# The second FFN's output as seven half-size products over pairs of features

## The chip, the cores and the metric

One core of a Trainium2 chip runs the kernel. The metric is the device time of one execution in microseconds (us); of the kernel before it is 911.15 us, the median of three runs (910.92 to 911.19). The engines are TensorE (PE, matrix products, with its weight loads shown as PEld), VectorE (DVE), ScalarE (ACT), GpSimd (POOL) and SyncE (SP), which issues nearly all transfers.

## The reference

Attention over a window of 64 positions, an FFN with ELU, and an RMS-normalized gated FFN, all in float32, on 2304 tokens of width 512:

```python
x = attention(q, k, v)                 # 4 batches, 8 heads, 576 positions, head width 64
h = x @ w_in                           # 512 -> 2048
g = np.where(h > 0.0, h, np.exp(np.minimum(h, 0.0)) - 1.0)
x = g @ w_out                          # 2048 -> 512
xn = x / np.sqrt(np.mean(x * x, axis=-1, keepdims=True) + 1e-06) * rms_g
g = xn @ w_gate                        # 512 -> 1536
silu = g * (1.0 / (1.0 + np.exp(-g)))
out = (silu * (xn @ w_val)) @ w_out2   # 1536 -> 512
```

## The kernel before

Products run in float32r, a rounded float32. To keep float32's accuracy each operand is split into a high part and a low part (the rest), and a product of two operands is three matmuls: high by high, high by low, low by high. A split is a copy with rounding (ACT or DVE) and a subtraction (DVE or POOL).

**First FFN.** Tokens go in five blocks (384, 384, 512, 512, 512). For each of 16 features f of 128, in_steps computes h (12 matmuls, L704) and g, and out_steps adds g's share to four accumulators (12 matmuls, L781), two steps later (LAG). Attention for later blocks runs between these steps. While blocks 1 to 3 run, prep_steps reads w_gate and w_val, forms the sums that the second FFN needs, splits them (put_out) and stores them in DRAM (pspill). prep_out does the same for w_out2 without sums: 12 features, one matrix each, two splits of 256 columns each, six in the last block and six in the first superblock (ospill). norm_steps normalizes a finished block.

**Second FFN.** Three superblocks (sb) of 768 tokens, in two token blocks of 384. pair(sb, i) computes g for features i and i + 6 at once: a 2x2 by 2x2 block product with Winograd's seven products instead of eight (ORDER), each for gate and value (qi), six matmuls of 384 columns each (L1106). The results are collected in SBUF (keep on ACT, L1061; plus on DVE, L1066), multiplied (times, L1070) and split into high and low (L1092, L1094). After three pairs, outs(sb, h) multiplies the g of six features with w_out2, plainly: for each of six token tiles of 128, six features and three terms, so 108 matmuls of 512 columns (L1148), four features first and the last two after. emit1 copies the first half's accumulators to SBUF (L1294), emit2 adds the second half's to them (L1300) and stores the rows (L1302). x_items forms the sums and splits of x for the next superblock.

**Order.** Every operation is a step with costs per engine that are written by hand, what it reads and writes, and the tile it needs. Plan runs a list scheduler over all steps: among the steps that could start first on an engine it takes the one with the longest chain of costs behind it (tail). Its order on each engine is then fixed, SP's transfers too. Places per tile kind are in LIMITS; of the kind "wu" (32 places of 4 KB per partition) are first the first FFN's weights and then x, g, the loaded sums of w_gate and w_val (p_load, 512 KB each) and w_out2 (o_load). A transfer is put into the program at a numbered point of its superblock (put, after).

Of the kernel before, what the change touches and what calls it, by code (L numbers as in the profile page):

```python
# [8 lines left out]
F32 = mybir.dt.float32  # L9
# [12 lines left out]
LIMITS = dict(w=4, c=6, e2=3, y=4, wu=32, kT=1, kq=1, vw=2, s=2, st=3, e=2, g=3, x0=1, x1=1, xt=1,  # L22
# [7 lines left out]
class Plan:  # L30
# [9 lines left out]

    def add(self, costs, fn, reads=(), writes=(), load=0.0, rows=128, name=None):
        x = Step()
        x.costs = {e: c * self.MARGIN.get(e, 1.0) for e, c in costs.items()}
# [67 lines left out]
    def could(self, x, e):  # L111
# [6 lines left out]
        for tile in x.tiles:  # L118
            if tile not in self.live and tile[0] in LIMITS:
                new.setdefault(tile[0], set()).add(tile)  # L120
# [15 lines left out]
    def put(self, x, e, t):  # L136
        c = x.costs[e]
        for tile in x.tiles:
            tag = tile[0]
            if tile not in self.live:  # L140
                self.live[tile] = len(self.users[tile])
                if tag in LIMITS:
                    if self.used.get(tag, 0) < LIMITS[tag]:
                        self.used[tag] = self.used.get(tag, 0) + 1
                    else:
                        self.freed[tag].remove(min(self.freed[tag]))
# [10 lines left out]
        for tile in x.tiles:  # L157
            self.live[tile] -= 1
            if not self.live[tile]:
                self.freed.setdefault(tile[0], []).append(  # L160
                    max(self.end[u] for u in self.users[tile]))
        self.order.append((x, e))

    def run(self, given=()):
# [13 lines left out]
        while ready:  # L178
# [36 lines left out]
def kernel(  # L215
# [459 lines left out]
    def load_step(f, i, tile):  # L675
        add({"SP": 0.55}, lambda e: f.load(i + 1), writes=[tile], load=1.45,
# [258 lines left out]
    def put_out(dst, dkey, src, key, sg):  # L935


        def tile_():
            return get((*sg, 0), lambda: mp.tile(
                [128, 2, 256], F32R, tag="stg", name="stg", bufs=2))  # L940
# [3 lines left out]
        add({"POOL": 0.76}, lambda e: nc.gpsimd.tensor_tensor(  # L944
# [5 lines left out]
    def prep_steps(t):  # L950

        i, qi = t // 2, t % 2
        raw = [("big4", ("r", 2 * t + j), 0) for j in range(2)]
        m = [(f"wm{j}", ("p", 2 * t + j)) for j in range(2)]
# [8 lines left out]
        for j in range(2):  # L963
            load_step(fwp, 2 * t + j, raw[j])
        for j in range(2):
            def join(e, j=j):
                held[(*m[j], 0)] = fwp.join(2 * t + j)
            add({"POOL": 0.8}, lambda e, j=j: fwp.s1(2 * t + j), reads=[raw[j]], writes=[one])
# [3 lines left out]
        def comb(out, okey, in0, in1, keys, op=ALU.subtract):  # L972
            add({"POOL": 0.76}, lambda e: nc.gpsimd.tensor_tensor(
                out=out(), in0=in0(), in1=in1(), op=op), reads=keys, writes=[okey])
# [3 lines left out]
        def put(j, src, key):  # L978
            put_out(pspill[:, 7 * i + ORDER.index(j), qi * 512:(qi + 1) * 512]
                    .rearrange("p (a c) -> p a c", a=2), ("dram", ("p", 7 * i + ORDER.index(j)), qi),  # L980
                    src, key, ("stg", (t, j)))

# [12 lines left out]
    def prep_out(j):  # L995

        n, f = 4 * NP2 + j, OF[j]
        raw, m = ("big4", ("r", n), 0), (f"wm{n % 2}", ("p", n))
        one = ("wm2", "top", 0)

        def join(e):
            held[(*m, 0)] = fwp.join(n)

        load_step(fwp, n, raw)
        add({"POOL": 0.8}, lambda e: fwp.s1(n), reads=[raw], writes=[one])
        add({"DVE": 0.75}, join, reads=[raw, one], writes=[(*m, c) for c in range(2)])
        for h in range(2):
            put_out(ospill[:, f, :].rearrange("p (a c) -> p a c", a=2)
                    [:, :, h * 256:(h + 1) * 256], ("dram", ("o", f), h),
# [350 lines left out]
```

## Time and profile before

| | us |
|---|---|
| median of three runs (lowest to highest) | 911.15 (910.92 to 911.19) |
| the profiled execution | 911.7 |
| its span, first to last instruction | 909.3 |
| PE busy | 896.3 (99%) |
| DVE busy | 547.9 (60%) |
| ACT busy | 460.5 (51%) |
| POOL busy | 227.5 (25%) |
| matmuls of the output phases (L1148), 648 of them | 103.0 + 52.9 |
| matmuls of the pairs (L1106), 1512 of them | 121.1 + 80.9 + 40.7 + 40.3 |

The profile is one execution, taken in hardware. Busy is the union of an engine's records; the records of matmuls overlap, since one begins before the one ahead has drained, so a matmul's own duration (390 ns for 512 columns) is longer than its share of the time. [...]

### The profile page before, as it was taken

Reading aid. Unit: us, or ns where it says so; the run is one execution under the profiler, and the core shown is the slowest. Engines: PE = TensorE matmul, PEld = TensorE weight load, DVE = VectorE, ACT = ScalarE, POOL = GpSimd, SP = SyncE. Lnnn points to the kernel's source line nnn. Section 1 sums busy time; section 2 is a strip of 40 time slices with the busy share of each in tenths; the row PEclk is TensorE's granted clock in tenths of the full one; section 3 lists DMA queues with packets and bytes.
Section 4 is the critical chain, followed back from the end, with each engine's and each line's share of the span. In section 5 each row is a group of like instructions: output and inputs, shape, how many; then the busy total and the mean of one; then the engine's idle time right before and its main releaser. Section 6 shows DMA issues by size and latency. Waiting matters only on the chain.

```text
span 909.3 us, 15448 instructions
## 1 busy us (share of the span) xinstructions
PE 896.3 (99%) x5577; PEld 805.8 (89%) x5577; DVE 547.9 (60%) x1188; ACT 460.5 (51%) x1118; POOL 227.5 (25%) x270
## 2 busy tenths in 40 slices
PE   8899999999999999999999999999999999999998
PEld 7889999998887888888888998998998998998996
DVE  6899967656555557557744781694560584560561
ACT  6788676666556665657445542451432451432430
POOL 3777631434434442344142013100000000000000
PEclk9999999999999999999999999999999999999999
DMA  9996226844385453945595529978947638847611
GB/s 228 324 325 155 58 82 184 221 129 140 122 240 145 142 151 106 254 141 160 200 353 176 199 72 338 367 276 322 338 139 270 210 112 314 310 140 272 214 48 69
DMA packets 149915, 182.89 MB, mean 201 GB/s; under 512 B 81744, under 2 KB 109392, under 8 KB 149840
## 3 DMA queue, kind: packets, MB, share of 16 engines
q1 hardware_dynamic: 149840, 181.91, 62.3%
q8 instruction: 44, 0.72, 0.3%
q14 instruction: 31, 0.25, 0.1%
HBM read 144.13 MB, written 37.75 MB: 200 GB/s over the span
## 4 chain that ended last, share of the span: by engine, by line
PE 88%; DMA 3%; DVE 3%; SPq 3%; ACT 1%; issue 1%; POOL 0%; DVEq 0%; ACTq 0%; POOLq 0%
PE y L781 19%; PE w L704 18%; PE y L1106 16%; PE w L1106 12%; PE y L1148 11%; PE w L1148 5%; SPq L308 2%; PE w L534 2%; PE w L455 1%; SPq L642 1%; PE w L519 1%; DVE wm L655 1%; PE w L400 1%; DMA kq<-in_q_dram 1%; DMA big<-in_moe_w_val_dram 1%
## 5 line engine op out<-in xcount | busy, mean ns | idle before, releaser
L781 PE MATMUL y<-g,wu 128*128 128x512 f32 (+1 forms) x960 | 213.5, 372 | 2.5 <-POOL wu L671 1.7
L704 PE MATMUL w<-x,wu 128*128 128x512 f32 (+1 forms) x960 | 213.0, 372 | 0.8 <-ACT x L559 0.5
L704 PEld LDWEIGHTS w<-x,wu 128*128 128x128 f32 x960 | 173.4, 188 | 26.1 <-issue 2.2
L781 PEld LDWEIGHTS y<-g,wu 128*128 128x128 f32 x960 | 173.0, 188 | 26.1 <-POOL wu L671 2.1
L1106 PE MATMUL y<-xw,pu 128*128 128x384 f32 x648 | 121.1, 334 | 0.0
L1066 DVE TENSOR_TENSOR c<-c,w 128x384 f32<-128x384 f32 x72 | 39.9, 554 | 133.5 <-PE w L1106 128.7
L1106 PEld LDWEIGHTS y<-xw,pu 128*128 128x128 f32 x648 | 113.2, 188 | 0.5 <-issue 0.2
L1148 PE MATMUL y<-wu,g 128*128 128x512 f32 x432 | 103.0, 390 | 0.0
L1148 PEld LDWEIGHTS y<-wu,g 128*128 128x128 f32 x432 | 81.0, 188 | 16.6
L944 POOL TENSOR_TENSOR stg<-wm,stg 128x256 fp32r<-128x256 f32 x72 | 58.8, 817 | 127.2 <-ACT stg L942 127.2
L1106 PE MATMUL w<-xw,pu 128*128 128x384 f32 x432 | 80.9, 334 | 0.0
L746 DVE SCALAR_TENSOR_TENSOR e<-e,w 128x512 f32<-128x512 f32 (+1 forms) x80 | 50.3, 631 | 50.5 <-ACT e L744 50.1
L752 DVE TENSOR_TENSOR g<-e,g 128x512 fp32r<-128x512 f32 (+1 forms) x80 | 66.1, 828 | 22.9 <-ACT g L750 22.4
L1106 PEld LDWEIGHTS w<-xw,pu 128*128 128x128 f32 x432 | 75.4, 188 | 0.1
L742 ACT ACTIVATE e<-w 128x512 f32<-128x512 f32 (+1 forms) x80 | 44.2, 552 | 61.5 <-PE w L704 60.5
L1061 ACT COPY c<-y 128x384 f32<-128x384 f32 x72 | 34.4, 479 | 59.8 <-PE y L1106 58.6
L648 POOL CAST top<-big 128x512 f16<-128x512 bf16 x36 | 29.6, 821 | 126.1 <-DMA big<-in_moe_w_out_dram 68.5
L1084 ACT ACTIVATE e<-c 128x384 f32<-128x384 f32 x54 | 28.4, 526 | 63.1 <-DVE c L1066 62.9
L1070 DVE TENSOR_TENSOR e<-e,c 128x384 f32<-128x384 f32 x108 | 59.3, 562 | 0.5
L1148 PE MATMUL w<-wu,g 128*128 128x512 f32 x216 | 52.9, 389 | 0.0
L671 POOL TENSOR_TENSOR wu<-wm,wu 128x512 fp32r<-128x512 f32 x32 | 49.4, 1566 | 13.8 <-ACT wu L666 10.7
L750 ACT CAST g<-e 128x512 fp32r<-128x512 f32 (+1 forms) x73 | 42.0, 577 | 20.9 <-DVE e L746 20.5
(132 smaller groups left out, 1213.8 us busy)
## 6 DMA issues: line engine op xcount, KB each, us to landing
pu<-pspill SPq DMA_DIRECT2D x126, 512.0 KB, 5.6
pspill<-stg SPq DMA_DIRECT2D x84, 256.0 KB, 2.1
wu<-ospill SPq DMA_DIRECT2D x36, 512.0 KB, 4.1
tmp<-in_moe_w_out_dram SPq DMA_DIRECT2D x16, 511.8 KB, 8.3
tmp<-in_moe_w_in_dram SPq DMA_DIRECT2D x16, 511.0 KB, 7.9
vw<-in_v_dram SPq DMA_DIRECT2D x27, 256.0 KB, 4.2
ospill<-stg SPq DMA_DIRECT2D x24, 256.0 KB, 4.5
big<-in_moe_w_out_dram SPq DMA_DIRECT2D x12, 511.8 KB, 5.3
```

The costliest lines, as they stand in the source:

```text
L671: nc.gpsimd.tensor_tensor(out=u[:, 1, :], in0=m, in1=u[:, 0, :].bitcast(F32), op=ALU.subtract)
L704: nc.tensor.matmul(pt[:, :n], lhsT=wt[:, a, kk * 128:(kk + 1) * 128], rhs=xs[kk][:, c, :n], start=(i == 0), stop=(i == len(seq) - 1))
L742: add({"ACT": of_n(0.49, n)}, lambda e: nc.scalar.activation(out=et(), in_=ph(), func=AF.Relu, scale=-1.0), reads=ws, writes=[e_])
L746: add({"DVE": of_n(0.56, n)}, lambda e: nc.vector.scalar_tensor_tensor(out=et(), in0=et(), scalar=-1.0, in1=ph(), op0=ALU.add, op1=ALU.max ...
L750: lambda e: copy_on(e)(out=gt()[:, 0, :n], in_=et()),
L752: add({"DVE": of_n(0.68 if b else 0.93, n)}, lambda e: nc.vector.tensor_tensor(out=gt()[:, 1, :n], in0=et(), in1=gt()[:, 0, :n].bitcast(F3 ...
L781: nc.tensor.matmul(py[m][:, :n], lhsT=wt[:, a, m * 128:(m + 1) * 128], rhs=g[:, c, :n], start=(first and i == 0), stop=(last and i == 2))
L944: add({"POOL": 0.76}, lambda e: nc.gpsimd.tensor_tensor(out=tile_()[:, 1, :], in0=src(), in1=tile_()[:, 0, :].bitcast(F32), op=ALU.subtrac ...
L1066: add({"DVE": 0.55}, lambda e: nc.vector.tensor_tensor(out=c_of(ck), in0=c_of(ck), in1=at(bk), op=ALU.add), reads=[bk], writes=[ck])
L1070: add({"DVE": 0.55}, lambda e: nc.vector.tensor_tensor(out=et(), in0=et(), in1=src_of(sk), op=ALU.mult), reads=[sk], writes=[ek])
L1106: nc.tensor.matmul(at(bk), lhsT=p_of(sb, i, j)[:, qi, a, kk * 128:(kk + 1) * 128], rhs=X_of(sb, j, kk)[:, x, :], start=(first and n == 0), ...
L1148: nc.tensor.matmul(at(m), lhsT=g[:, a, (m % 3) * 128:(m % 3 + 1) * 128], rhs=w[:, x, :], start=(f == fs[0] and i == 0), stop=(f == fs[-1] ...
```

## The change

- The output phase outs multiplies by seven products too. The 2x2 blocks are features i and i + 6 by the two token blocks (g), and features by the two halves of 256 output columns (w_out2). For each of the seven products j, in ORDER, a sum or difference of blocks of g is formed (source, 0 or 1 subtraction per pair), split (split), and multiplied: three token tiles, three pairs, three terms, 27 matmuls of 256 columns, as two steps (q): two token tiles in a bank of tag y, the third in one of tag w. Accumulators are shared along the products as in pair, and each step's result is collected at once (keep, plus). g itself is kept whole in float32, and pair no longer splits it.
- Differences and low parts may go to DVE (cost 0.56) or POOL (1.2). Sums for even products sit in the three places of tag g, for odd ones in three of big4 (in the first half of the first superblock in wu). The steps on a pair's g are ready as soon as that pair's g is, so during the next pair.
- prep_out now forms w_out2's seven sums of quarters per pair of features and splits and stores them (44 places of 256 KB instead of 24 stores). Four pairs come in the last block of the first FFN, two in the first superblock.
- o_load loads two such sums at a time, 11 loads per half instead of 6. Loaded weights (p and o) get their own limit of 8 of wu's 32 places.
- The planner takes, of DVE and POOL, the engine that would end a step sooner; preparation and normalization get a higher priority (sooner); accumulators of tag y are given out in order.
- Results are collected per half of columns and stored as 256 or 128 tokens by 256 columns, eight stores per superblock instead of six.

The core of the diff:

```diff
-LIMITS = dict(w=4, c=6, e2=3, y=4, wu=32, kT=1, ...
+LIMITS = dict(w=4, c=6, e2=3, y=4, wu=32, wl=8, kT=1, ...
...
     def queue(self, t):
         if t[0] == "wu":
-            return "raw" if t[1][0] == "r" else "wu" if isinstance(t[1], tuple) else None
+            return ("raw" if t[1][0] == "r" else "wl" if t[1][0] in ("p", "o") else
+                    "wu" if isinstance(t[1], tuple) else None)
+        if t[0] == "y" and isinstance(t[1][0], int):
+            return "y"
         return None if t[0] in "wy" else t[0]
+    def tags(self, t):
+        return (t[0], "wl") if self.queue(t) == "wl" else (t[0],)
...
                 can = {e: self.could(x, e) for e in x.costs}
+                if len(can) == 2 and "POOL" in can and "DVE" in can and can["DVE"] is not None:
+                    e = min(can, key=lambda e: can[e] + x.costs[e])
+                    can = {e: can[e]}
...
-                        per.setdefault(e, []).append((t, -self.tail[x.index], x.index))
+                        per.setdefault(e, []).append((t, -self.tail[x.index] - x.early, x.index))
...
     def pair(sb, i, after):
...
             times(ek, et, sk)
-            f, blk = i + NP2 * (pos // 10 - 1), pos % 10 - 1
...
-            add({"ACT": 0.52, "DVE": 0.42}, lambda e: copy_on(e)(
-                out=g_of(gkey)[:, 0, :], in_=et()), reads=[ek], writes=[(*gkey, "h")])
-            add({"DVE": 0.56}, lambda e: nc.vector.tensor_tensor(
-                out=g_of(gkey)[:, 1, :], in0=et(), in1=g_of(gkey)[:, 0, :].bitcast(F32),
-                op=ALU.subtract), reads=[ek, (*gkey, "h")], writes=[(*gkey, "l")])
...
-        for m in range(NM):
-            mm(m, fs[:-2])
-            after()
-        for m in range(NM):
-            mm(m, fs[-2:])
-            emit(m, po[m], lambda m=m: at(m))
-            after()
+    def outs(sb, h, after, emit):
+        us = [3 * h + ii for ii in range(3)]
...
+        def minus(o, x, y):
+            add({"DVE": 0.56, "POOL": 1.2}, lambda e: on(e).tensor_tensor(
+                out=o[0](), in0=x[0](), in1=y[0](), op=ALU.subtract),
+                reads=[v[1] for v in (x, y) if v[1] != o[1]], writes=[o[1]])
+        def S_key(jp, i, part):
+            return (("g", "wu" if sb + h == 0 else "big4")[jp % 2], ("S", sb, i, jp), part)
...
+        def split(jp, i, src):
+            add({"ACT": 0.52, "DVE": 0.42}, lambda e: copy_on(e)(
+                out=S_of(jp, i)[:, 0, :], in_=src[0]()),
+                reads=[src[1]], writes=[S_key(jp, i, "h")])
+            add({"DVE": 0.56, "POOL": 1.2}, lambda e: on(e).tensor_tensor(
+                out=S_of(jp, i)[:, 1, :], in0=src[0](),
+                in1=S_of(jp, i)[:, 0, :].bitcast(F32), op=ALU.subtract),
+                reads=[src[1], S_key(jp, i, "h")], writes=[S_key(jp, i, "l")])
+        def source(j, i):
+            if j == 5:
+                minus(G(i, 0, 0), G(i, 0, 1), G(i, 0, 0))
+            elif j == 6:
+                minus(t2(i), G(i, 1, 1), G(i, 0, 0))
+            elif j == 7:
+                minus(G(i, 0, 1), G(i, 1, 1), G(i, 0, 1))
+            elif j == 4:
+                minus(G(i, 1, 0), G(i, 1, 0), t2(i))
+            return {1: G(i, 0, 0), 5: G(i, 0, 0), 6: t2(i), 2: G(i, 1, 0), 7: G(i, 0, 1),
+                    3: G(i, 1, 1), 4: G(i, 1, 0)}[j]
...
+        for jp, j in enumerate(ORDER):
+            for i in us:
+                split(jp, i, source(j, i))
+            for q in range(2):
...
+                    for m in ((0, 1), (2,))[q]:
+                        for ii, i in enumerate(us):
+                            w = o_of(sb, o_entry(i, j))
+                            for n, (a, x) in enumerate(((0, 0), (0, 1), (1, 0))):
+                                nc.tensor.matmul(
+                                    at(bk)[:, (m % 2) * 256:(m % 2) * 256 + 256],
+                                    lhsT=S_of(jp, i)[:, a, m * 128:(m + 1) * 128],
+                                    rhs=w[:, x * 256:(x + 1) * 256],
...
+                add({"PE": (2.16, 1.08)[q]}, product, reads=reads, writes=[bk])
+                emit(j, q, bk, (lambda bk=bk: at(bk)))
+                after()
...
+    PREP = [{}, *[{f: 4 * b + n for n, f in enumerate((3, 6, 9, 12))}
+              for b in range(nblk - 2)],
+            {5: 12, 8: 13, 11: 14, 13: 15}]
...
+        def emit1(j, q, bk, at, keep=keep, plus=plus):
+            (plus if j in (2, 7, 3) else keep)(STEP[j][0], q, bk, at)
+        def emit2(j, q, bk, at, plus=plus, store=store):
+            plus(STEP[j][0], q, bk, at)
+            if STEP[j][1]:
+                store(STEP[j][0], q)
```

## Rows read from the trace of the kernel before

**Rows 1.** The page: span, and TensorE's busy time, share and instructions.

```profile
span 909.3 us, 15448 instructions
...
PE 896.3 (99%) x5577; PEld 805.8 (89%) x5577; DVE 547.9 (60%) x1188; ACT 460.5 (51%) x1118; POOL 227.5 (25%) x270
```

**Rows 2.** Windows: busy us and instructions per engine, granted clock, DMA share, GB/s.

```profile
410.00:492.00 82.00, 82.00 (x362) 67.51 (x361) 52.40 (x80) 44.32 (x86) 27.03 (x31) 1.00 0.63 215
495.00:632.00 137.00, 137.00 (x723) 127.96 (x722) 86.96 (x161) 57.81 (x123) 14.74 (x18) 1.00 0.74 263
562.00:606.00 44.00, 44.00 (x253) 43.52 (x252) 26.75 (x53) 22.07 (x49) 5.73 (x7) 1.00 0.97 358
632.00:769.00 137.00, 137.00 (x724) 128.42 (x723) 69.83 (x137) 49.23 (x103) 0.00 (x0) 1.00 0.66 230
769.00:905.00 136.00, 136.00 (x720) 127.58 (x719) 59.35 (x116) 42.84 (x88) 0.00 (x0) 1.00 0.52 182
```

**Rows 3.** TensorE's timeline, one output phase: start us, duration us, engine, line, op.

```profile
605.82 2.24 PE L1106 MATMUL y<-x,pu 128*128 128x384 f32 x12
607.90 2.92 PE L1148 MATMUL y<-wu,g 128*128 128x512 f32 x12
610.66 2.88 PE L1148 MATMUL w<-wu,g 128*128 128x512 f32 x12
613.38 2.88 PE L1148 MATMUL y<-wu,g 128*128 128x512 f32 x12
...
632.42 1.75 PE L1106 MATMUL y<-xw,pu 128*128 128x384 f32 x9
```

**Rows 4.** The page, costliest groups: count, busy us, mean ns of one, idle before.

```profile
L1148 PE MATMUL y<-wu,g 128*128 128x512 f32 x432 | 103.0, 390 | 0.0
...
L1148 PE MATMUL w<-wu,g 128*128 128x512 f32 x216 | 52.9, 389 | 0.0
...
L1148 PEld LDWEIGHTS y<-wu,g 128*128 128x128 f32 x432 | 81.0, 188 | 16.6
```

**Rows 5.** TensorE's timeline, transposes and the product after them.

```profile
161.08 1.03 PE L519 MATMUL w<-ident,s 128*128 128x128 f32 x8
161.96 0.60 PE L400 MATMUL w<-ident,kq 128*128 128x128 f32 x4
162.31 2.33 PE L704 MATMUL w<-x,wu 128*128 128x384 f32 x12
```

**Rows 6.** Timeline of the weight loads in the same stretch.

```profile
162.28 2.04 PEld L704 LDWEIGHTS w<-x,wu 128*128 128x128 f32 x12
```

**Rows 7.** VectorE's timeline, a dense stretch; nine operations from first to last start.

```profile
613.08 1.02 DVE L902 TENSOR_TENSOR xw<-slot,xw 128x384 fp32r<-128x384 f32 x2
...
617.30 1.02 DVE L909 TENSOR_TENSOR slot<-slot,slot 128x384 f32<-128x384 f32 x2
```

**Rows 8.** Groups of VectorE from 495 to 909 us: count, busy us, mean ns.

```profile
L1300 DVE TENSOR_TENSOR slot<-slot,y 128x512 f32<-128x512 f32 x12 | 8.3, 688 | 33.3 <-PE y L1148 33.3
...
L655 DVE SCALAR_TENSOR_TENSOR wm<-big,top 128x512 int32<-128x512 int32 x6 | 4.1, 690 | 12.8 <-POOL top L648 8.1 <-POOL stg L944 4.6
...
L839 DVE SCALAR_TENSOR_TENSOR big<-big,g_sb,big 128x512 f32<-128x512 f32 x4 | 3.9, 987 | 0.0
```

**Rows 9.** Groups of GpSimd, whole span.

```profile
L944 POOL TENSOR_TENSOR stg<-wm,stg 128x256 fp32r<-128x256 f32 x72 | 58.8, 817 | 127.2 <-ACT stg L942 127.2
L671 POOL TENSOR_TENSOR wu<-wm,wu 128x512 fp32r<-128x512 f32 x32 | 49.4, 1566 | 13.8 <-ACT wu L666 10.7 <-DMA kq<-in_k_dram 3.1
```

**Rows 10.** Groups of VectorE, 26 to 185 us (only L746 reads PSUM).

```profile
L752 DVE TENSOR_TENSOR g<-e,g 128x384 fp32r<-128x384 f32 x30 | 28.4, 953 | 5.9 <-ACT g L750 5.7
L746 DVE SCALAR_TENSOR_TENSOR e<-e,w 128x384 f32<-128x384 f32 x30 | 16.3, 548 | 10.6 <-ACT e L744 10.4
```

**Rows 11.** DMA issues from 495 to 909 us: count, KB, median us to landing.

```profile
pu<-pspill SPq DMA_DIRECT2D x109, 512.0 KB, 6.0
wu<-ospill SPq DMA_DIRECT2D x36, 512.0 KB, 4.1
```

**Rows 12.** Timeline of the end: last matmuls and the last add.

```profile
902.61 2.88 PE L1148 MATMUL y<-wu,g 128*128 128x512 f32 x12
...
905.53 0.69 DVE L1300 TENSOR_TENSOR slot<-slot,y 128x512 f32<-128x512 f32 x1 [0.67 <-PE y L1148]
```

More of the change, by code (lines that the diff above doesn't have):

```diff
@@ L119, in could @@
             if tile not in self.live and tile[0] in LIMITS:
-                new.setdefault(tile[0], set()).add(tile)
+                for tag in self.tags(tile):
+                    new.setdefault(tag, set()).add(tile)
         for tag, ts in new.items():
@@ L981, in put, with sums, comb @@
                     src, key, ("stg", (t, j)))
+        sums(q4, k4, both, sk, put, {"POOL": 0.82})
+    def sums(q4, k4, both, sk, put, cost):
+        def comb(out, okey, in0, in1, keys, op=ALU.subtract):
+            add(cost, lambda e: on(e).tensor_tensor(
+                out=out(), in0=in0(), in1=in1(), op=op), reads=keys, writes=[okey])
         put(1, q4[0, 0], k4[0, 0])
@@ L1235 @@
             if f == 4:
-                next(norm, None)
+                plan.sooner(100.0, lambda: next(norm, None))
             if f < F1:
@@ L1242 @@
                 attention(u, b=max(i for i in range(nblk) if FIRST_U[i] <= u))
-            if b and f in (3, 6, 9, 12) and not last:
-                prep_steps((b - 1) * 4 + (3, 6, 9, 12).index(f))
+            if f in PREP[b]:
+                kind, i = preps[PREP[b][f]]
+                plan.sooner(40.0, lambda: (prep_steps if kind == "p" else prep_out)(i))
             for fn in slots.get(f, ()):
@@ L1278 @@
             next(norm)
-            put(4, lambda: next(norm, None))
-            for j in range(F2 // 2, F2):
-                put(6 + 2 * (j - F2 // 2), lambda j=j: prep_out(j))
+            put(2, lambda: plan.sooner(100.0, lambda: next(norm, None)))
+            for i in range(4, NP2):
+                put(2 * (i - 4), lambda i=i: plan.sooner(0.0, lambda: prep_out(i)))
         if sb + 1 < NSB:
-            put(36, lambda: x_load(sb + 1))
+            put(38, lambda: x_load(sb + 1))
             for j, fn in enumerate(x_items(sb + 1)):
-                put(48 + j, fn)
+                put(50 + j, fn)
@@ new lines, in keep, with plus @@
+        def keep(pos, q, bk, at, sb=sb, part=part, p_key=p_key):
+            n = (512, 256)[q]
+            add({"ACT": (0.59, 0.38)[q], "DVE": (0.69, 0.42)[q]}, lambda e: copy_on(e)(
+                out=part(pos, q), in_=at()[:, :n]), reads=[bk], writes=[p_key(pos, q)])
+        def plus(pos, q, bk, at, sb=sb, part=part, p_key=p_key):
+            n = (512, 256)[q]
+            add({"DVE": (0.69, 0.42)[q]}, lambda e: nc.vector.tensor_tensor(
+                out=part(pos, q), in0=part(pos, q), in1=at()[:, :n], op=ALU.add),
+                reads=[bk], writes=[p_key(pos, q)])
@@ new lines, in store @@
+        def store(pos, q, sb=sb, part=part, p_key=p_key):
+            tok, c = 2 * NB * sb + NB * (pos % 10 - 1) + 256 * q, 256 * (pos // 10 - 1)
+            n = (256, 128)[q]
+            add({"SP": 0.55}, lambda e: nc.sync.dma_start(
+                out=out[tok:tok + n, c:c + 256].rearrange("(m p) c -> p m c", p=128),
+                in_=part(pos, q).rearrange("p (m c) -> p m c", c=256)),
+                reads=[p_key(pos, q)], load=0.7)
+        STEP = {1: (11, 0), 5: (22, 0), 6: (12, 0), 2: (11, 1), 7: (22, 1), 3: (12, 1), 4: (21, 1)}
```

227 lines of the change are left out of this document (124 added, 103 removed).

## The prediction

> **What bounds the kernel now.** I read the page first. TensorE (PE) is busy 896.3 of 909.3 us [rows 1], but busy time is an average over stages, so the next view was the windows of the stage that is changed, the second FFN from about 495 us on. In each of the three parts of that stage PE is busy for the whole window (137.00 of 137.00), at the full granted clock (1.00, the 2.4 GHz level), while VectorE (DVE) has 87.0, 69.8 and 59.4 us of work and ScalarE (ACT) 57.8, 49.2 and 42.8 [rows 2]. The last block of the first FFN, in which most of the new preparation is placed, is as full: 82.00 of 82.00 [rows 2]. So matmul time taken out of the second FFN comes off the end one for one, unless PE has to wait for something it does not wait for now. The rest of the argument is the price of the new matmuls, and then who could be late.
>
> **The matmuls.** A half's output phase now runs from 607.90 to 632.42 us: 24.52 us [rows 3] for 108 matmuls of 512 columns (648 in six halves, [rows 4]), and in its steady part 12 of them take 2.72 us (610.66 to 613.38), 226.7 ns each. Twelve of 384 columns in the pair before it take 2.08 us (605.82 to 607.90), 173.3 ns each [rows 3]. The two lie on a line of 53.3 ns per 128 columns, so 256 columns should cost 120.0 ns. The change issues 7 products x 3 token tiles x 3 pairs x 3 terms = 189 matmuls a half: 22.68 us. That is 1.84 us less per half and **11.0 us less in all**. Only that: an eighth of the streaming (648 x 213.3 ns = 138.2 us) is 17.3, and the 13.3 ns that the line leaves at zero columns, paid 1134 times instead of 648, takes 6.5 of it back; the first matmuls of a phase, a little dearer now, make up the difference.
>
> No row shows a 256-column product of this type, so I bound it. Every matmul has a weight load of its own, and its record lasts 188 ns [rows 4]. Were that the time for which the loader is taken, the price would be 188, and the change would add 1134 x 188 - 147100 ns = 66 us. But the loads of the pairs already come every 173.3 ns, so the record is longer than the load. Closer is what happens after transposes, whose products follow each other every 108 ns (eight take 1.03 us, four 0.60): the last four end at 162.56, the weights of the next product begin to load at 162.28, under the last transpose [rows 6], and the twelve products of 384 columns behind them end at 164.64, exactly 12 x 173.3 ns after the transposes [rows 5]. A load of 128 columns is thus hidden behind a product of 108 ns, and a product of 256 columns lasts 120. I take 120.0, with 120 to 126 in the range (6 ns is what reading two-digit starts can hide), worth 0 to +6.8 us. [...]
>
> **The work of VectorE.** Dense, DVE starts a 384-column operation every 0.469 us (613.08 to 617.30, nine of them), although each record lasts 0.55 [rows 7]; an operation of 512 columns lasts 0.688 [rows 8], so about 0.60 dense, and one of 256, by the same line, 0.33. Per superblock (768 tokens) the splits of g go from 24 to 42 and 24 differences are new: 42 x 0.469 = 19.7 us. Collecting the sums goes from 6 adds of 512 columns (3.6 us) to ten of 512 and ten of 256 (9.3): +5.7. DVE comes to 69.8 + 25.4 = 95 us in a superblock of 133. The 18 added copies on ACT are hidden (49 + 9 of 133). On average all of it is covered; places where it is not:
> - *The opening, pairs 0 to 2 and the first output phase, 66 us.* DVE has 42 operations of pairs (19.7), 33 of sums and splits (15.5), the normalization of the last block with four at 0.99 and twelve at 0.69 (12.2), four joins at 0.69 (2.8) [rows 8] and the collecting (2.8): 53 us. Fits by 13. Beside it GpSimd (POOL) has the last two preparations of w_out, 13 operations each, about 0.82 us apiece [rows 9]: 21 us.
> - *The boundary between superblocks, pair 5, second output phase, next pair 0, 52 us.* 28 operations of pairs (13.1), 23 sums and splits that could not begin earlier (10.8), collecting and adding (6.5), 22 for the next x (10.3): 41 us. Fits by 11.
>
> Here the planner's new rule matters: a sum or a low half goes to POOL whenever POOL would end it sooner. POOL's price for 384 columns lies between 0.817 (256) and 1.566 (512) [rows 9], by the line about 1.19, and it is not free for DVE. While POOL was busy, in the first blocks, the subtraction with two SBUF inputs took 953 ns on average, and the operation of the same width with one input in PSUM 548 [rows 10]. So POOL's operations hold up DVE's lows, differences and multiplications, not its adds out of PSUM. [...] If DVE waited out all of POOL's 21 us in the opening it would be 7 us over; waiting for half of them (POOL spends the other half waiting for ACT's copies) it just fits. At a boundary, 11 of the 33 sums on POOL take 5.2 us from DVE and add 13.1 of lock: 49 of 52. The three splits of a product take some 2 us, and they may begin when the product two before it ends, 27 x 0.120 = 3.24 us ahead; the last is not read until 0.7 us into its product. So about 2 us of lateness goes unseen. I charge **+3 us of PE waits**: 2 in the opening, 0.5 at each boundary; ends 0 and 17 (below).
>
> **Preparation.** Per pair, w_out now takes four combinations and seven splits beside two casts: 13 x 0.82 = 10.7 us of POOL instead of 4.9, and 7 stores instead of 4. Four pairs come in the last block, where POOL is busy 27 of 82 us and DVE 52 [rows 2]. It costs nothing while PE there has the two steps of lag between a product of g and its use; without that cover a wait of DVE behind POOL, up to 0.8 us, would show per step. The higher priority of preparation and normalization only reorders ready steps. Together 0, between -1 and +2.
>
> **Transfers.** A superblock streams 42 loads of 512 KB for the pairs as before, and 21 instead of 12 such loads for the output, plus 3.1 MB of x and results: 36.2 MB in 133 us, 272 GB/s. The stage already ran at 358 GB/s from 562 to 606 us with PE at 44.00 of 44.00 [rows 2]. Eight places hold six loads beyond those being read, 12.5 us at one per 2.08, against a landing of 6.0 us in the median [rows 11]. SyncE (SP) issues 76 instead of 64 transfers per superblock; a store that waits for a late add holds up the loads queued behind it, but by no more than the lateness itself. Cost 0.
>
> **The end.** The last adds and store follow the last matmul: the add of 0.69 at 905.53 and then a store [rows 12]. The new last add has 256 columns and its store half the bytes: -0.3 us.
>
> **Sum.** The profiled execution took 911.7 us, 2.4 around its span of 909.3 [rows 1]. 911.7 - 11.0 + 3 - 0.3 = 903.4; the median of the runs, 911.15, stands 0.55 lower, which gives 902.9. A measurement of this kernel tells about 0.2% (1.8 us) from no change.
>
> **Rivals.**
> - *Waits eat the gain.* Same mechanism as the charge above, three to four times as large: some 11 us, spread over opening and boundaries, and the time is 911. For it: the opening fits by little. Chance 0.10.
> - *POOL's lock turns VectorE into the bound (slower).* The place is the second output phase with its pair 5, 37.3 us: 6.6 + 10.8 + 6.5 + 10.3 = 34.2 us of DVE; 11 operations moved to POOL make it 34.2 - 5.2 + 13.1 = 42.1, 4.8 over, at two boundaries 9.6; the opening adds its 7. With 16.6 us of waits the time is 902.9 - 3 + 16.6 = 916.5. It decides once the waits pass 11.3 us. For it rows 10; against it, adds out of PSUM don't wait, the next pair 0 has 5 us to give, and the plan may send less to POOL. Chance 0.15.
> - *The weight load shows.* Above 129.7 ns a product the matmuls save nothing (147.1 / 1134); 140 ns makes it 926, the record's 188 makes it 980. Against it rows 5 and 6. Chance 0.03. [...]
> - *The early sums don't happen.* Only three places of g and three others hold split sums, so only the first two of seven products can be ready; if pair 2's results come late the phase opens with a wait of some 2 us, six times: +12, about 915. It would need the pair's last multiplications late too. Chance 0.04.
> - *No waits at all* is the low end of the forecast: 899.9.
>
> **Numbers.** Forecast, with waits of 0 to 8 us: 899 to 908, chance 0.68, all of it faster. Waits that eat the gain are the 0.10 of no change; the lock (0.15), the load (0.03) and the early sums (0.04) make 0.22 slower. The range of 8 in 10 takes in the lock's 916.5: 899 to 917.
>
> **What would show it.** Right: matmuls of 256 columns every 120 ns, six output phases of 22.7 us, PE idle under 4 us in the second FFN. Waits of PE for DVE or POOL at the sums, subtractions near 1 us while POOL is busy, would show the lock; starts 130 ns apart without a wait, the load; PE waits for the streamed weights, the eight places. I am wrong if PE's idle time passes 9 us, or if the first FFN's blocks change by over 2.

## The result, and the profile after

The changed kernel takes **916.21 us** (median of four runs, 915.95 to 917.68), the kernel before 911.07 (910.92 to 911.19) beside it: a ratio of 1.006 (95% interval 1.0042 to 1.0077). It is slower, where 902.9 and faster was forecast; the time lies inside the range of 899 to 917. The profiled execution took 915.95.

The page of the changed kernel: span and busy time of each engine.

```profile
span 914.2 us, 16974 instructions
...
PE 891.2 (97%) x6063; PEld 824.5 (90%) x6063; DVE 632.4 (69%) x1294; ACT 489.3 (54%) x1191; POOL 345.9 (38%) x379
```

TensorE is busy for 5.1 us less than in [rows 1], in a span that is 4.9 longer: 10 us of new idle time. The windows of the second FFN (columns as in [rows 2]) say where.

```profile
495.00:632.00 137.00, 129.90 (x791) 126.84 (x792) 104.45 (x165) 67.95 (x151) 71.56 (x76) 0.96 0.79 290
632.00:769.00 137.00, 136.55 (x914) 136.35 (x913) 99.32 (x182) 58.33 (x126) 28.86 (x25) 1.00 0.74 265
769.00:905.00 136.00, 136.00 (x912) 136.00 (x911) 92.88 (x175) 52.05 (x111) 24.95 (x21) 1.00 0.70 251
```

From 632 us on PE is full but for 0.45 us, as forecast. The loss lies before: PE is busy for 129.90 of 137.00 us, at a granted clock of 0.96 where [rows 2] has 1.00. A clean output phase of the changed kernel, on TensorE's timeline, shows the new matmuls:

```profile
688.32 2.31 PE L1237 MATMUL y<-wu,g 128*128 128x256 f32 x18
...
691.55 2.32 PE L1237 MATMUL y<-wu,big 128*128 128x256 f32 x18
...
710.99 1.21 PE L1141 MATMUL y<-xw,pu 128*128 128x384 f32 x6
```

A product's 27 take 3.23 us (688.32 to 691.55), the 189 of the phase 22.67: 120 ns each, and 1.85 us less than the 24.52 of [rows 3]. The gain is there. Set out by the starts of the stages (first matmul of each, from the timelines; us from the start of the span):

| | pair 0 | 1st output phase | 2nd | 3rd | 6th | end of span |
|---|---|---|---|---|---|---|
| before | 495.1 | 539.7 | 607.9 | 676.1 | 880.8 | 909.3 |
| after | 501.3 | 546.2 | 620.1 | 688.3 | 888.1 | 914.2 |

So 6.2 us are lost before the second FFN begins. From the first to the second output phase another 5.7 are lost, and as the shorter matmuls should have made this stretch 1.8 shorter, the loss there is 7.5. From the third phase on the changed kernel wins back 7.3.

**The first loss.** TensorE's timeline at the end of the first FFN; in brackets the idle time ahead and what ended it.

```profile
472.11 2.88 PE L729 MATMUL w<-x,wu 128*128 128x512 f32 x12
...
485.71 2.88 PE L806 MATMUL y<-g,wu 128*128 128x512 f32 x12
489.41 3.02 PE L806 MATMUL y<-g,wu 128*128 128x512 f32 x12 [0.83 <-ACT g L775]
496.01 5.49 PE L806 MATMUL y<-g,wu 128*128 128x512 f32 x12 [3.58 <-ACT g L775]
501.30 1.58 PE L1141 MATMUL w<-xw,pu 128*128 128x384 f32 x6
```

From 485.71 on, three lots of 12 matmuls take 15.6 us instead of 8.2 (36 x 226.7 ns): 4.4 us are waits for g of the last two features, and the last lot runs at half speed (5.29 us instead of 2.72). The windows give the granted clock: 0.57 from 495 to 503 us, around the end of the longer wait, and 0.50 from 495.5 to 502 alone, where it was 1.00 before. (No run shows the 2.4 GHz that the prediction puts beside 1.00; what [rows 3] give there is 128 columns in 53.3 ns, 2.4 a ns.)

```profile
495.00:503.00 8.00, 6.99 (x20) 5.84 (x21) 3.30 (x5) 2.22 (x5) 6.41 (x9) 0.57 0.29 108
553.00:557.00 4.00, 4.00 (x23) 4.00 (x22) 2.01 (x4) 0.99 (x2) 1.89 (x4) 0.57 0.17 66
```

Why is g late? ScalarE and GpSimd are idle shortly before. The chain begins with feature 13. ScalarE has the Relu of feature 13 (L767) in its line behind a copy of a prepared sum of w_out2 (L972). The h that the Relu reads was done by 475.0 (the matmuls of 472.11, 2.88 long), and it runs at 481.06, 6.1 us late; the features behind it inherit the delay. Their timelines:

```profile
480.75 0.41 ACT L972 CAST stg<-wm 128x256 fp32r<-128x256 f32 x1 [8.53 <-DMA ospill<-stg]
481.06 0.59 ACT L767 ACTIVATE e<-w 128x512 f32<-128x512 f32 x1
...
481.24 0.74 POOL L974 TENSOR_TENSOR stg<-wm,stg 128x256 fp32r<-128x256 f32 x1 [12.09 <-ACT stg L972]
```

The copy waits 8.5 us for a place of stg, the kind of tile in which a sum waits to be stored. There are two such places, so the copy waits for a store. SyncE's timeline shows what stands ahead of the stores:

```profile
459.88 5.37 SPq L977 DMA_DIRECT2D ospill<-stg  x3
465.29 7.34 SPq L663 DMA_DIRECT2D tmp<-in_moe_w_out_dram  x4
...
475.02 0.33 SPq L663 DMA_DIRECT2D tmp<-in_moe_w_out_dram  x1
475.44 0.86 SPq L977 DMA_DIRECT2D ospill<-stg  x2
477.74 3.05 SPq L663 DMA_DIRECT2D tmp<-in_moe_w_out_dram  x2
482.00 20.30 SPq L977 DMA_DIRECT2D ospill<-stg  x10
```

and its waits from 455 to 490 us say for what:

```profile
SPq L977 <- POOL stg L974: 16.6, 8, 3.1
SPq L663 <- PE w L729: 6.0, 3, 2.3
SPq L663 <- PE y L806: 4.7, 3, 2.3
```

The loads at L663 bring raw w_out2 into tmp, places of wu that TensorE's first FFN is still reading. Six of them wait until PE leaves one, 10.7 us in all, and finished sums stand behind them. By the code only the four loads for pairs 4 and 5 go to tmp. But nothing in the plan orders the loads, so it has those of pairs 4 and 5 ahead of loads for pairs 2 and 3, and the helper that issues a load issues every one with a lower number first, into the same kind of place. So seven loads went to tmp. The first line of these waits, 16.6 us of stores waiting for POOL, could also mean that POOL has too much to do; but POOL itself is idle for 12.09 us in the middle, and e5 and e7 below decide it.

**The second loss.** TensorE's timeline in the first output phase:

```profile
546.22 2.31 PE L1237 MATMUL y<-wu,g 128*128 128x256 f32 x18
548.37 1.24 PE L1237 MATMUL w<-wu,g 128*128 128x256 f32 x9
549.62 0.50 PE L1237 MATMUL y<-wu,g 128*128 128x256 f32 x2
551.24 0.62 PE L1237 MATMUL y<-wu,g 128*128 128x256 f32 x3 [1.12 <-DVE g L1202]
552.52 2.56 PE L1237 MATMUL y<-wu,g 128*128 128x256 f32 x13 [0.66 <-DVE g L1202]
554.88 3.12 PE L1237 MATMUL y<-wu 128*128 128x256 f32 x18
557.84 1.24 PE L1237 MATMUL w<-wu 128*128 128x256 f32 x9
...
561.21 2.18 PE L1237 MATMUL y<-wu 128*128 128x256 f32 x16 [0.80 <-DVE wu L1202]
...
578.35 1.34 PE L1237 MATMUL w<-wu,g 128*128 128x256 f32 x9 [2.13 <-DVE slot L1399]
```

There are four waits, 4.7 us in all: three for split sums and one for a collection, each late on VectorE. From 553 us PE runs at about half the clock again (0.57 in the second row of the windows above, 0.50 from 553.5 to 556.5). The product behind the first (j = 1) is j = 6, not 5 as in ORDER; both 1 and 6 have their sums in the three places of g.

What made the collection (L1399) late can be read from VectorE's timeline, with GpSimd's next operation below it:

```profile
571.10 1.39 DVE L860 SCALAR_TENSOR_TENSOR big<-e,big 128x512 f32<-128x512 f32 x1
...
575.09 0.69 DVE L860 SCALAR_TENSOR_TENSOR big<-e,big 128x512 f32<-128x512 f32 x1
...
577.88 0.75 DVE L1399 TENSOR_TENSOR slot<-slot,w 128x256 f32<-128x256 f32 x2
```

```profile
579.89 1.23 POOL L669 CAST top<-tmp 128x512 f16<-128x512 bf16 x1 [5.38 <-DVE wm L676]
```

From 568.54 to 577.96 VectorE does nothing but nine operations of the last block's normalization (L855, L857, L860), which has a higher priority now, and the collection stands behind them. Until GpSimd falls idle at 574.5 they take 1.10 to 1.40 us each, then 0.69: five long ones cost some 3 us more, so here GpSimd holds VectorE up.

### The profile page after: what moved, and what is told of

It is laid out like the page before. It is cut to its first block, busy times and chain, and to the rows that moved or that the text cites. A ratio compares the mean times of both kernels' runs of the same rounds, so it can differ in the third digit from the quotient of the medians.

```text
span 914.2 us, 16974 instructions
## 1 busy us (share of the span) xinstructions
PE 891.2 (97%) x6063; PEld 824.5 (90%) x6063; DVE 632.4 (69%) x1294; ACT 489.3 (54%) x1191; POOL 345.9 (38%) x379
## 4 chain that ended last, share of the span: by engine, by line
PE 85%; DVE 7%; DMA 3%; ACT 3%; issue 1%; POOL 1%; SPq 0%; DVEq 0%; POOLq 0%; ACTq 0%
PE w L729 19%; PE y L806 19%; PE y L1141 16%; PE w L1141 12%; PE y L1237 8%; PE w L1237 4%; PE w L555 2%; PE w L476 2%; PE w L540 1%; PE w L421 1%; DVE wm L676 1%; DMA ospill<-stg 1%; DVE g L1202 1%; DVE g L777 1%; DMA kq<-in_k_dram 1%
## 5 line engine op out<-in xcount | busy, mean ns | idle before, releaser
L806 PE MATMUL y<-g,wu 128*128 128x512 f32 (+1 forms) x960 | 216.9, 376 | 7.0 <-ACT g L775 4.4
L1202 POOL TENSOR_TENSOR g<-slot,g 128x384 fp32r<-128x384 f32 x21 | 27.0, 1286 | 151.9 <-ACT g L1199 108.2
L767 ACT ACTIVATE e<-w 128x512 f32<-128x512 f32 (+1 forms) x80 | 44.2, 552 | 57.8 <-PE w L729 57.0
L974 POOL TENSOR_TENSOR stg<-sw,stg 128x256 fp32r<-128x256 f32 x50 | 40.8, 817 | 77.9 <-ACT stg L972 77.9
L1118 DVE TENSOR_TENSOR slot<-slot,c 128x384 f32<-128x384 f32 x108 | 64.0, 604 | 0.9
L1237 PE MATMUL y<-wu,g 128*128 128x256 f32 x432 | 57.8, 287 | 3.6 <-DVE g L1202 3.4
L1237 PEld LDWEIGHTS y<-wu,g 128*128 128x128 f32 x432 | 54.8, 194 | 4.8 <-DVE g L1202 4.2
L1129 ACT ACTIVATE slot<-c 128x384 f32<-128x384 f32 x54 | 28.4, 526 | 52.0 <-DVE c L1114 50.6
```

The source lines that it names most:

```text
L767: add({"ACT": of_n(0.49, n)}, lambda e: nc.scalar.activation(out=et(), in_=ph(), func=AF.Relu, scale=-1.0), reads=ws, writes=[e_])
L806: nc.tensor.matmul(py[m][:, :n], lhsT=wt[:, a, m * 128:(m + 1) * 128], rhs=g[:, c, :n], start=(first and i == 0), stop=(last and i == 2))
L974: add(cost, lambda e: on(e).tensor_tensor(out=tile_()[:, 1, :], in0=src(), in1=tile_()[:, 0, :].bitcast(F32), op=ALU.subtract), reads=[key ...
L1118: add({"DVE": 0.55}, lambda e: nc.vector.tensor_tensor(out=et(), in0=et(), in1=src_of(sk), op=ALU.mult), reads=[sk], writes=[ek])
L1237: nc.tensor.matmul(at(bk)[:, (m % 2) * 256:(m % 2) * 256 + 256], lhsT=S_of(jp, i)[:, a, m * 128:(m + 1) * 128], rhs=w[:, x * 256:(x + 1) * ...
```

## The experiments

All ratios are to the kernel before on the same chip, with the 95% interval; the kernel after is 1.006 (1.0042 to 1.0077). The runs below were taken on three chips, where the kernel before has medians of 911.0 to 912.3, so compare ratios where they are close. Each edit lets the scheduler order all steps anew, so a difference in time need not come from the place that was edited; the starts of the stages say where it arose. Line numbers shift by a few where an edit adds lines.

**Four ways to relieve the preparation and VectorE.** Every other sum of the last block staged in places of wu beside stg's two (e1):

```diff
+            if sg[0] == "wu":
+                return get((*sg, 0), unit)[:, :, 0:256]
...
-                    ("e" if i >= 4 and ORDER.index(j) % 2 else "stg", ("o", i, j)), EITHER)
+                    ("stg", ("o", i, j)) if ORDER.index(j) % 2 == 0 else
+                    ("e", ("o", i, j)) if i >= 4 else ("wu", f"so{i}{j}"), EITHER)
```

> Edit: in the last block every other prepared sum of w_out2 is staged in a place of its own in wu instead of in one of the two of tag stg. Theory staging (ScalarE's copies stand ahead of g's chain and wait for a staging place until its store has landed, so PE starves at the end of the first FFN and its clock falls): the 7.4 us lost between 485.7 and 501.3 us fall to 2 or less, total about 910 to 911. Theory lock (POOL's subtractions hold VectorE and are what makes g late): staging is not the wait, and with POOL fed faster the loss stays or grows, 915 to 918.

Measured: 910.01 us, 0.9976 (0.996 to 0.9991). Pair 0 still begins at 500.1, against 501.3: more staging alone does not remove the first loss. Of the 4.5 us by which the profiled span is shorter (909.7 for 914.2), 1.2 are gained by then, the rest later.

The priority of preparation taken away (e2):

```diff
-    plan.sooner(40.0, lambda: (prep_steps
+    plan.sooner(0.0, lambda: (prep_steps
```

> Edit: preparation gets no priority (40 becomes 0), normalization keeps its 100. Theory staging: g's chain is placed ahead of the copies on ScalarE, the loss at the end of the first FFN is mostly gone (under 2 us of 7.4), total 909 to 911, unless preparation slips into the second FFN and costs there. Theory lock: the amount of POOL work is the same, so the loss stays within 2 us of what it is, 914 to 917.

Measured: 929.34, 1.0181 (1.0158 to 1.0204). Pair 0 begins at 505.7, with 6.6 us of waits for g ahead of it, and nine loads went to tmp. So the first loss does not need the priority.

Sums and low parts on VectorE alone (e3), the test of what the prediction calls the lock, that VectorE is held up while GpSimd works:

```diff
-            add({"DVE": 0.56, "POOL": 1.2}, lambda e: on(e).tensor_tensor(
+            add({"DVE": 0.56}, lambda e: on(e).tensor_tensor(
```

(in minus and in split.)

> Edit: the differences of g and the low parts of their splits may go to VectorE alone. Theory lock: the waits of the output phases of the first superblock (7.4 us in the stretch 546 to 620, 1.9 in the next output phase) fall to 3 or less together, total 909 to 911, with the end of the first FFN unchanged. Rival (preparation and normalization crowd VectorE and GpSimd there, not the sums): VectorE only gets more to do, the waits stay or grow, 915 to 919.

Measured: 927.64, 1.0153 (1.0122 to 1.0185). VectorE is held up less. Its groups from 500 us on, first of the kernel after, with over 60 sums and low parts on POOL (L1118, times, multiplies by an operand in SBUF, c, or in PSUM, y; L1202 forms low parts):

```profile
L1118 DVE TENSOR_TENSOR slot<-slot,c 128x384 f32<-128x384 f32 x108 | 64.0, 604 | 0.9
...
L1202 DVE TENSOR_TENSOR g<-slot,g 128x384 fp32r<-128x384 f32 x31 | 20.5, 705 | 0.0
...
L1118 DVE TENSOR_TENSOR slot<-slot,y 128x384 f32<-128x384 f32 x36 | 19.7, 548 | 0.9
```

then of e3, without them:

```profile
L1118 DVE TENSOR_TENSOR slot<-slot,c 128x384 f32<-128x384 f32 x108 | 61.7, 582 | 2.8 <-ACT slot L1129 1.9
...
L1202 DVE TENSOR_TENSOR g<-slot,g 128x384 fp32r<-128x384 f32 x48 | 26.8, 587 | 0.7 <-ACT g L1199 0.6
...
L1118 DVE TENSOR_TENSOR slot<-slot,y 128x384 f32<-128x384 f32 x36 | 19.8, 550 | 0.9
```

The low parts fall from 705 to 587 ns, the multiplications by c from 604 to 582, while those with an input in PSUM stay at 548 and 550. Single operations of the kernel after show the same. With GpSimd idle, the low part of 756.33 us (L1202) takes 0.55; the one of 759.99 takes 1.38 and ends at 761.37, 0.42 behind GpSimd's operation of 759.56, which lasts 1.39; the multiplication by y of 761.29 takes 0.54 beside GpSimd's next (761.21, 1.03 long).

If every operation on two inputs in SBUF were held up so, POOL's help would be worth nothing. The time refutes that: without this help PE waits 8.4 us for sums, as its waits in e3 say, three times some 3 us.

```profile
PE y L1237 <- ACT g L1199: 8.4, 3, 3.0
```

(The wait is put down to ScalarE's copy, which came last. Why that copy came late was not followed up.)

Preparation moved earlier, five matrices per block in blocks 1 to 3 and one in the last (e4):

```diff
-    PREP = [{}, *[{f: 4 * b + n for n, f in enumerate((3, 6, 9, 12))}
-              for b in range(nblk - 2)],
-            {5: 12, 8: 13, 11: 14, 13: 15}]
+    PREP = [{}, *[{f: 5 * b + n for n, f in enumerate((2, 5, 8, 11, 14))}
+              for b in range(nblk - 2)], {5: 15}]
```

> Edit: five preparations instead of four in each of blocks 1 to 3, so that three of the six pairs of w_out2 are done before the last block and one in it. Theory staging: the last block has 7 such copies instead of 28 and they end early, so the loss at the end of the first FFN is under 1 us; the last two pairs come sooner too, and the first output phases lose less: 903 to 909. Theory lock with the sums of g as its cause: the first output phases lose what they lose now, about 9 us, total 908 to 911. If blocks 1 to 3 can't cover five preparations, PE waits there and the gain is given back, 912 or more.

Measured: 935.59, 1.025 (1.0227 to 1.0272). TensorE's waits:

```profile
PE y L806 <- ACT big L839: 23.4, 3, 8.6
```

These are output products at the start of a block, waiting until the last block's accumulators are copied out to big, which is also where raw matrices are loaded. That these two collided for places is my reading and was not tried by itself. Moved this way, the preparation is not covered in the earlier blocks either.

**The order of SyncE's loads.** All loads of matrices for preparation write one common key, so the plan keeps them in the order of their numbers (e5); the same with e1's staging (e6):

```diff
-        add({"SP": 0.55}, go, writes=[tile], load=1.45,
+        add({"SP": 0.55}, go, writes=[tile] + ([] if f is fw1 else [(("dram", "feed", 0), 50.0)]), load=1.45,
```

> Edit: the loads of raw weights for the preparation are kept in their order by the planner, so the loads of the last two pairs (into wu) can't be put ahead of those of pair 2 and 3 (into big4), which the helper then loads early into wu as well, unplanned. Theory SP queue (those loads wait for places of wu that PE frees, finished sums wait behind them to be stored, so staging stays full, ScalarE's copies wait with g's chain behind them): the waits of PE at 489 and 492 us and the half clock after them go, the 7.4 us lost before the second FFN fall to 1 or less, the sums of the last pairs come earlier and the first output phase loses less; total 902 to 908. Theory overload (POOL and VectorE can't do four pairs in the last block, whatever the order): the loss at the end of the first FFN stays above 4 us, total 911 to 917.

Measured: 912.4, 1.001 (0.9998 to 1.0022). The first loss is gone; SyncE's timeline of e5 no longer has loads to tmp ahead of the stores, and by TensorE's the last three lots of the first FFN take 8.16 us, without a wait.

```profile
474.70 11.33 SPq L977 DMA_DIRECT2D ospill<-stg  x5
...
486.87 1.36 SPq L663 DMA_DIRECT2D tmp<-in_moe_w_out_dram  x3
```

```profile
485.61 8.32 PE L806 MATMUL y<-g,wu 128*128 128x512 f32 x36
493.77 1.23 PE L1141 MATMUL w<-xw,pu 128*128 128x384 f32 x6
```

Pair 0 begins 7.5 us sooner than in the kernel after; 3.4 of it is lost again by the second output phase. The first now waits 1.1, 1.9 and 0.3 us for sums and, further on, 2.9 for which the trace names no cause. The nine operations of the normalization are there again: they end at 570.37, the collection behind them at 570.96, and PE goes on at 571.07.

> Edit: the order of loads as in the run before, and every other sum staged in wu as in the run with more staging. Theory SP queue: staging is not short once stores are issued on time, so within 2 us of the order alone. Theory staging: another 2 us or more below it.

Measured: 905.94, 0.9938 (0.9923 to 0.9953): 0.6% faster than the kernel before.

The rival way to keep those loads from PE's places, all raw matrices in big4 (e7, without the common key):

```diff
-raw = [("wu", ("ro", n), 0) if i >= 4 else ("big4", ("r", n), 0) for n in ns]
+raw = [("big4", ("r", n), 0) for n in ns]
```

> Edit: the raw weights of the last two pairs go through big4 like the others, so no load can overtake another. Theory SP queue: the loss at the end of the first FFN is under 1.5 us, as with the order kept; the last two pairs share big4 with the normalization of the last block and come later, so waits in the first output phases may be longer: 903 to 911. Theory overload: 911 to 917.

Measured: 915.43, 1.0039 (1.0025 to 1.0052). Pair 0 begins at 494.4: the first loss goes this way too, so its cause was the loads' waiting for wu. Now sums come late in the first two output phases (waits of up to 4.1 us).

> Edit: the order of loads kept, and the differences and low parts of the sums of g on VectorE alone. Theory lock (POOL's share of the sums costs more than it gives): at or below the time of the order alone. Rival (VectorE needs POOL's help in the output phases): 8 us or more above it, with PE waits at the sums in the second output phase of superblocks 0 and 1, as in the earlier run with the sums on VectorE.

e8 joins the edits of e5 and e3: 917.85, 1.0071 (1.005 to 1.0093), 5.5 us above e5. Without the first loss too, POOL's share is worth more than the time for which it holds VectorE up.

**The first output phase.** Taken on e6: normalization without its priority (e9: put(2, ...) without sooner), POOL's price raised to 1.6 so that less goes there (e10), both (e11), and six places for streamed weights instead of eight (e12: wl=6).

> Edit: on top of the order of loads and the staging in wu, the normalization of the last block (in the first superblock) loses its priority of 100. Theory crowd (its twelve operations, 0.7 to 1.4 us each, stand on VectorE just ahead of the last collection of pair 2, so g comes late to the first output phase): the wait of 2.0 us at 544 and the half clock after it go, total 900 to 904. Theory lock (POOL's 63 operations on the sums slow VectorE there): the wait stays within 1 us, total 904 to 908. If the normalization slips into the second output phase and holds big4's places there, the wait appears there instead.

> Edit: on top of the order of loads and the staging in wu, POOL's cost of a difference or low part is 1.6 instead of 1.2 in the plan, so it gets 44 of them instead of 63. Theory lock: VectorE is held up less, the first output phase loses less, total 901 to 904. Theory crowd: the normalization still stands ahead of pair 2's collection, no gain, 905 to 910.

> Edit: both (no priority for the normalization, POOL at 1.6 with 41 operations on the sums). Theory crowd: as without the priority alone, within 2 us. Theory lock: as POOL at 1.6 alone, within 2 us. If both add, 898 to 901, which is what the matmuls alone would give.

> Edit: on top of the order of loads and the staging in wu, streamed weights get six places of wu instead of eight. If the transfers are covered as predicted (four loads ahead are 8.3 us against about 6 to land), within 2 us of the time with eight, 904 to 908. If the eight places only just suffice, PE waits for pu or wu transfers in the pairs, 910 or more.

Measured: e9 906.13 (0.9944, 0.993 to 0.9957), e10 906.01 (0.9945, 0.9933 to 0.9958), e11 906.09 (0.9942, 0.993 to 0.9955), e12 **902.9** (0.9914, 0.99 to 0.9929). Neither the norm's priority nor POOL's share of the sums (44 operations for 63) removes the wait in front of the second product: 2.7, 1.9, 2.3 and 2.0 us, in e6 2.0. This does not clear the norm itself: five of its nine operations still stand ahead of that wait in e9. Nor did any run take the last two preparations off POOL there. In e12 no wait of PE for a streamed weight appears, so six places are enough. Of the 3.2 us by which e12's profiled span is shorter than e6's, 1.2 are gained before pair 0 and 2.0 from the first to the second output phase. The latter shows in two pairs of lines; first e6's timeline, then e12's:

```profile
546.17 3.56 PE L1240 MATMUL y<-wu,g 128*128 128x256 f32 x16 [2.00 <-DVE g L1205]
549.56 1.24 PE L1240 MATMUL w<-wu,g 128*128 128x256 f32 x9
```

```profile
544.83 2.39 PE L1240 MATMUL y<-wu,g 128*128 128x256 f32 x16 [1.99 <-DVE g L1205]
547.06 1.24 PE L1240 MATMUL w<-wu,g 128*128 128x256 f32 x9
```

The same wait, but behind it e6 takes 3.39 us for 16 matmuls and e12 2.23. The clock fell in one and not in the other (from 545 to 550 us it is 0.66 in e6 and 1.00 in e12); two smaller waits of e6 (0.8 and 0.4) are gone as well. Each is one execution, and the times of a kernel spread by as much: 902.24 to 905.59 in e12, 905.03 to 907.91 in e6, with mean granted clocks of 0.996 to 0.998 in both. So it is not shown that the six places are what kept the clock up.

**Was it the order of the products?** The sums take their places of wu in a fixed order with the other users of wu (queue), and get theirs late. So the sums were taken out of that order: on e12 (e13), with eight places (e14), with e5's edit alone (e17) and on the kernel after alone (e18).

```diff
     def queue(self, t):
...
+            if t[1][0] == "S":
+                return None
             return ("raw" if t[1][0] == "r" else "wl"
```

> Edit: order of loads kept, staging in wu, six places for streamed weights, and the split sums of g taken out of the ordered queue for places of wu. Theory product order: no wait over 0.7 us in the first output phase, total 899 to 901.5. Theory VectorE late: a wait of 2 us or more stays there under another product, 902 to 905.

> Edit: order of loads, staging in wu, sums out of the queue, eight places as in the changed kernel. Theory product order: 4 to 6 us below the run with order and staging alone (905.9), 900 to 902. Theory VectorE late: 904 to 907.

> Edit: order of loads and sums out of the queue, staging as in the changed kernel. Theory product order: the waits of 1.1 and 1.9 us at 543 to 545 of the run with the order of loads alone go, 6 us or more below its 912, 902 to 906. Theory VectorE late: 909 to 913.

> Edit: on the changed kernel alone, the sums of g out of the queue. Theory product order: the waits of the first output phase (1.1, 0.7, 0.8 us and the half clock) go, the loss before the second FFN stays, 908 to 912. Theory VectorE late: 914 to 918.

Measured: e13 903.45 (0.9909, 0.9896 to 0.9922), e14 905.21 (0.9931, 0.9918 to 0.9944), e17 912.08 (1.0006, 0.9998 to 1.0015), e18 917.89 (1.007, 1.0058 to 1.0083). PE's order is 1, 5, 6 again, but the time is no better than without the edit: e13 against e12, e17 against e5, e18 against the kernel after. The wait has only moved. TensorE's timeline of e13, just ahead of its first output phase, where VectorE has the nine operations of the normalization from 529.03 to 538.84 and then the collection (L1119) that PE waits for:

```profile
539.83 2.37 PE L1146 MATMUL y<-x,pu 128*128 128x384 f32 x12 [2.73 <-DVE c L1119]
542.04 2.64 PE L1242 MATMUL y<-wu,g 128*128 128x256 f32 x18
```

and of e17 in its second, where without e6's staging a sum comes 6 us late:

```profile
622.37 3.43 PE L1239 MATMUL y<-wu,g 128*128 128x256 f32 x12 [6.04 <-ACT g L1201]
625.60 2.12 PE L1239 MATMUL w<-wu,g 128*128 128x256 f32 x9
```

The starts of the stages of the best versions beside e5:

| | pair 0 | 1st output phase | 2nd | 3rd | 6th | end of span |
|---|---|---|---|---|---|---|
| e5 | 493.8 | 539.9 | 616.0 | 684.2 | 884.0 | 910.1 |
| e6 | 495.4 | 540.0 | 611.5 | 677.9 | 877.6 | 903.7 |
| e12 | 494.2 | 538.8 | 608.2 | 674.6 | 874.4 | 900.5 |
| e13 | 494.5 | 542.0 | 609.3 | 675.7 | 875.5 | 901.5 |

e12 is 0.9% faster than before, and 13.3 us faster than the change as it was made.

## Why the prediction was wrong

- **The matmuls: right.** 120 ns each, 22.67 us a phase, 1.85 saved. From the third phase to the sixth the changed kernel takes 199.8 us where the kernel before takes 204.7. Each has a weight load of its own (6063 of both on the page), whose record lasts 192 to 216 ns on average, by tile; with 120 ns from start to start, loads and products overlap.
- **"Together 0" for the preparation: this step failed.** I priced its operations on POOL and DVE, and of SyncE only the second FFN's transfers. Their time was there: GpSimd's 12 and ScalarE's 8.5 us of idling fall in the middle of it. What I left out is that every sum leaves through two places of stg and a queue that issues in order, and that the moved loads of w_out2 go into places that PE has yet to leave. The stores waited behind them, the copies waited for the stores, g waited behind the copies. The loss is 7.4 us (15.6 for 8.2), against -1 to +2; e5 and e7 remove it in two ways. I named two steps of lag as the cover, against a wait of up to 0.8 us; the stall was one of 8.5 us. Up to there the first FFN was 1.2 us ahead of the kernel before.
- **The opening: right mechanism, wrong size.** I charged 2 us; from the first to the second output phase 7.5 is lost. Of these 4.7 are the waits, and 1.6 is what the 31 matmuls from 552.52 to 557.84 took beyond 120 ns each, at about half the clock, for which the sum had no term. The largest wait (2.1) came from the normalization, whose 12.2 us the sum spread over the 66 us of the opening, while the plan put nine of its operations in one block ahead of a collection. With the stores in order and staging to spare (e12) the same stretch takes 69.4 us, 3.0 over the clean 66.4, near the charge. A wait of 2 to 3 us stays whatever the order of the products, the priority of the normalization and POOL's share of the sums (e9 to e13). In e13 it stands behind the normalization; which of VectorE's jobs would have to go in the others was not found, and this stays open.
- **The boundaries: right kind, too small.** From the second phase to the third 1.8 us is lost (66.4 clean), from the third to the sixth 0.6. Charged were 0.5 each, 1.0 for two.
- **The lock as the slower rival: its time came true, 916.5 for 916.21, its reason did not.** That the time is met is luck. The rival wanted 9.6 us at two boundaries; they lost 2.4. Its 13.1 us let VectorE wait out each of eleven operations of POOL whole, which rows 10, means over 30 operations, don't show. In the kernel after a single one is waited out (1.38 us for 0.55, e3 above), but a low part takes 705 ns on average, 118 more than in e3. It gave the opening 7, where 7.5 is lost, and the lock has a share in that (some 3 us of the normalization's operations), but the first loss is no part of it. VectorE is held up, but taking the sums off POOL costs 5.5 us (e8) to some 10 (e3) more. The rival *waits eat the gain* fits the second FFN better: 9.9 us are lost in opening and boundaries, for its 11, and without the 6.2 before pair 0 the span would be 1.3 shorter than before.
- **Transfers, end: right.** PE never waits for a streamed weight; 265 GB/s in the middle superblock, against 272 worked out. From the start of PE's last matmul to the end of the span it takes 3.6 us (910.6 to 914.2) instead of 4.2 (905.1 to 909.3).
- **The sum:** -1.2 first FFN, +7.4 its end, +0.4 pairs 0 to 2, +7.5 the opening's phase, +2.4 boundaries, -11.0 matmuls, -0.6 end: +4.9, as the spans differ. Both signs that were to make me wrong came: PE has 10 us of new idle time, against "PE's idle time passes 9 us", and the first FFN ends 6.2 us later, against "over 2".

## What to carry to other kernels

When work is moved, follow each of its transfers down its queue: what a load waits for before it can be issued, and which finished results stand behind it. An engine that is half idle on average is no cover if the way out of it is two buffers deep. A scheduler orders only what is told to it: a helper that issues loads in a fixed sequence must appear in the plan as a dependency, and one line that says so was worth 4 to 5 us alone, and 13 with more staging and fewer places for streamed weights. And work that fits into a stretch by its sum can still stand as one block ahead of the result that is waited for.

## What the runs showed of the hardware that was not expected

A wait of TensorE cost well over its length: at the end of the 3.58 us wait the granted clock fell to one half (0.50 from 495.5 to 502 us, 0.57 on average from 495 to 503), and 12 matmuls took 5.29 us instead of 2.72; behind the 6.04 of e17, 12 of 256 columns took 3.23 instead of 1.44 (0.57 from 620 to 630). Not every wait did so: behind waits of 2.00 and 1.99 us, with the same work, the clock fell in e6 (0.66 from 545 to 550) and stayed at 1.00 in e12. What decides between them no run here shows.
